# Decode of float64 weights: the low word moved to ScalarE, the scaled word moved to PSUM, two biases written as numbers

## The chip, the cores and the metric

One core of one Trainium2 chip runs the whole program. The metric is the device time of one execution in microseconds (us). The kernel before took 1444.06 us, the median of three runs (1442.41 to 1444.91).

## The reference

Three stages follow one another on 8192 tokens of width 192. The first is a convolution whose seven taps per head come from a softmax; the second is an MLP with a rational activation; the third is an MLP with a hard-swish. The four weight matrices reach the kernel as float64.

```
w = exp(weight_gen - max);  w = w / (sum(w) + 1e-9)          # 2 x 4096 x 8 heads x 7 taps
x = sum over 7 taps of w * x shifted                         # 8192 x 192
h = x @ w_in                                                 # 192 -> 2048
P = a0 + a1*h + a2*h*h + a3*h*h*h
Q = 1 + |b0|*|h| + |b1|*h*h
x = (P / (Q + 1e-6)) @ w_out                                 # 2048 -> 192
h = x @ w_in2                                                # 192 -> 2048
out = (h * clip(h + 3, 0, 6) / 6) @ w_out2                   # 2048 -> 192
```

## The kernel before

The tokens are cut into 32 blocks of 256, and each block's 2048 hidden columns into four groups of 4 x 128. So there are 128 steps ("sl" in the code), and one step holds a 128x1024 tile of h in PSUM. TensorE (PE) multiplies; the elementwise work of a step is shared by VectorE (DVE), ScalarE (ACT) and GpSimd (POOL). For the first MLP a matrix is split into a high and a low half, so that three or five matmuls make one product.

One step of the first MLP goes: `in1` (PE, twenty matmuls, L258), `act_u`, `act_w`, `act_l` (ACT, L280 to L292), `pool_q` (POOL, L299), `dve_t` and `dve_t2` (DVE, L303 and L307), `act_ln`, `act_exp`, `act_q` (ACT, L314 to L323), `dve_hi` (DVE, L328), `pool_m` (POOL, L336), `dve_d` (DVE, L341), `pool_lo` (POOL, L349), `out1` (PE). The second MLP is `in2` (PE), `act_r2` (ACT, L393, a Relu), `dve_g2` (DVE, L399), `out2` (PE, L415). Between the two stand `mid_y` (ACT, L227) and `mid_f` (PE, L237).

Before that, and woven into the first steps, 28 jobs bring the weights in. A job loads a piece as pairs of 32-bit words into a tile `st` (SP, L433), 512 or 384 words wide per partition. `dec_scale` (L458, ACT) multiplies the high words by a power of two into a tile `dt`; `dec_low` (L465, DVE) turns the low word into its top three bits; `dec_join` (L471, DVE) shifts `dt` and ors the three bits in; `dec_sign` (L478, DVE) ors the sign in and writes `wf` (or, for the last matrix, `wo` itself). For three of the four matrices a "cut" follows: ACT rounds the high half (L487) and POOL or DVE subtracts it (L488). The 28 jobs are 12 of 512 words ("in" and "pair") and 16 of 384 words ("o1" and "o2").

The order on each engine is written out by a planner, `plan()` (L708): every operation has an engine or a choice of two, a cost, a due time and buffers that it takes (`take`), and the planner lists what would start first. Each engine then runs its list in that order, and an instruction that waits holds up all behind it. Buffers are rings: three `st`, three `wf`, two `dt`, two `h1` and two `h2` tiles in PSUM. A `st` buffer comes free after the job's sign, and the next load waits for that. `h2` is the PSUM ring of the second MLP and also of the transposes `xT` and of `yf`. When all 28 jobs have ended, the space of `st`, `wf` and `dt` is given to the tiles of the second MLP (`to_late`, L76): nothing of the second MLP starts before.

Of the kernel before, what the change touches and what calls it, by code (L numbers as in the profile page):

```python
# [8 lines left out]
F32 = mybir.dt.float32  # L9
F32R = mybir.dt.float32r  # L10
I32 = mybir.dt.int32
U32 = mybir.dt.uint32
AF = mybir.ActivationFunctionType
ALU = mybir.AluOpType
# [5 lines left out]
def kernel(  # L20
# [12 lines left out]
    nc = tc.nc  # L33
    P = 128
# [8 lines left out]
    NTB = SUB * P  # L43
# [9 lines left out]
    CEPS = 1.0 + 1e-6  # L53
# [9 lines left out]
    const = ctx.enter_context(tc.tile_pool(name="const", bufs=1))  # L63
# [4 lines left out]
    ps_h2 = ctx.enter_context(tc.tile_pool(name="ps_h2", bufs=2, space=PSUM))  # L68
# [4 lines left out]
    early = [stage.enter_context(tc.tile_pool(name="early", bufs=1))]  # L73
# [8 lines left out]
    acol = const.tile([P, 4], F32, name="acol")  # L82
    bcol = const.tile([P, 2], F32, name="bcol")
    bab = const.tile([P, 2], F32, name="bab")
    ceps = const.tile([P, 1], F32, name="ceps")
    half = const.tile([P, 1], F32, name="half")

    win = [
        {n: wts.tile([P, FF], F32R, name=f"win{i}{n}") for n in ("hi", "lo")} for i in range(2)
# [221 lines left out]
    def act_ln(sl):  # L311
        e = e1[sl]
        r = two.tile([P, GW], F32, tag="r0", name="r0")
        nc.scalar.activation(out=r, in_=e["w"], func=AF.Ln, bias=ceps[:, 0:1])  # L314
        e["r"] = r

    def act_exp(sl):
# [60 lines left out]
    h2 = {}  # L378
# [10 lines left out]
    def act_r2(sl, hh):  # L389
        r = late[0].tile([P, 2 * NTB], F32, tag="r2", name="r2")  # L390
        h = h2[sl, hh]
        r2[sl, hh] = r
        nc.scalar.activation(out=r, in_=h, func=AF.Relu, scale=1.0 / 6.0, bias=half[:, 0:1])  # L393

    def dve_g2(sl, hh):
        r, h = r2.pop((sl, hh)), h2.pop((sl, hh))
# [60 lines left out]

    def dec_scale(j):  # L458
        st = j["st"]
        j["y"] = early[0].tile([P, st.shape[1]], F32, tag="dt", name="dt", bufs=2)  # L460
        nc.scalar.activation(
            out=j["y"], in_=st[:, :, 1].bitcast(F32), func=AF.Copy, scale=2.0 ** -112
        )

    def dec_low(j):  # L465
        low = j["st"][:, :, 0]
        nc.vector.tensor_scalar(
            out=low, in0=low.bitcast(U32), scalar1=2.0 ** -29, scalar2=7.0, op0=ALU.mult, op1=ALU.min
        )

    def dec_join(j):  # L471
# [61 lines left out]
    def job_step(key, n, e=None):  # L533
        eng = nc.vector if e == "DVE" else nc.gpsimd
        if n == "load":
            kind, a = key[0], key[1:]
            j = {"in": job_in, "pair": job_pair, "o1": job_out1, "o2": job_out2}[kind](*a)
            job_load(j)
            jobs[key] = j
            return  # L540
        j = jobs[key]
        if n == "scale":
            dec_scale(j)
        elif n == "low":
            dec_low(j)
        elif n == "join":
            dec_join(j)
        elif n == "sign":
            dec_sign(j)
        elif n == "hi":  # L550
            j["cuts"] = j["cuts"](j["w"])
            for h, _ in j["cuts"]:
                h()
        else:
            for _, l in j["cuts"]:
                if l:
                    l(eng)
# [18 lines left out]
    def op(key, eng, cost, prio, emit, after=(), take=(), lat=0.15):  # L576
        choice = eng if isinstance(eng, tuple) else ((eng, cost, 0.0),)
        ops[key] = dict(
            key=key, choice=choice, prio=prio, emit=emit, after=after, take=take, lat=lat
        )  # L580
# [12 lines left out]
    for n, key in enumerate(order):  # L593
        p = JP0 + n * JPT - (30.0 if n < 2 else 0.0)
        f64, split = WS == 2, key[0] != "o2"
        sz = 1.0 if key[0] in ("in", "pair") else 0.75
        last = ("job", key, "lo" if split else "sign" if f64 else "load")
        wf = [("wf", 3, [last])] if split else []

        def step(k, eng, cost, prev, take=(), lat=0.15, also=[]):  # L600
            op(
                ("job", key, k), eng, cost, LOADP.get((n, k), p - LP * (k == "load")), lambda e=None, key=key, k=k: job_step(key, k, e),
                ([("job", key, prev)] if prev else []) + also, take, lat,
            )

        flex = (("POOL", 1.25 * sz, 0.0), ("DVE", 0.62 * sz, PEN))
        step("load", "SP", 1.46 * sz, None, [("st", 3, [("job", key, "sign")])] if f64 else wf, 2.2)
        if f64:
            step("scale", "ACT", 0.52 * sz, "load", [("dt", 2, [("job", key, "sign")])])
            step("low", "DVE", 0.34 * sz, "load")  # L610
            step("join", "DVE", 0.61 * sz, "scale", also=[("job", key, "low")])
            step("sign", "DVE", 0.61 * sz, "join", wf)
        if split:
            step("hi", "ACT", 1.6 if key[0] == "pair" else 0.52 * sz, "sign" if f64 else "load")
            step("lo", flex, 0, "hi")
        done[key] = last
# [37 lines left out]
    for sl in range(NS):  # L654
# [3 lines left out]
        for k in range(2):  # L658
            jobs_in = [done["in", 0, q], done["pair", 0, q // 2 * 2]]
            add("in1", "PE", 1.09, t + k, in1, sl, k,  # L660
                after=[("lo0", b)] + jobs_in + prev("in1", k),
                take=[("h1", 2, [("dve_d", sl)])] if k == 0 else [])
            add("out1", "PE", 1.09, t + 2 * T + 2.2 + k, out1, sl, k,
                after=[("pool_lo", sl), done["o1", 2 * q + k]] + prev("out1", k),
                take=[("y1", 1, [("lo1h", b)])] if q + k == 0 else [])
            jobs_in = [done["in", 1, q], done["pair", 1, q // 2 * 2]]
            t2 = t + 6 * T + (4.3, 8.1)[k]
            add("in2", "PE", 1.09, t2, in2, sl, k, after=[("lo1t", b)] + jobs_in,
                take=[("h2", 2, [("dve_g2", sl, k)])])
            t2 = t + 6 * T + (5.5, T + 0.7)[k]  # L670
            add("act_r2", "ACT", 0.57, t2, act_r2, sl, k, after=[("in2", sl, k)],
                take=[("r2", 2, [("dve_g2", sl, k)])])
            t2 = t + 6 * T + (7.9, T + 1.3)[k]
            add("dve_g2", "DVE", 0.6, t2, dve_g2, sl, k, after=[("act_r2", sl, k)] + prev("dve_g2", k),
                take=[("g2", 2, [("out2", sl, 1)])] if k == 0 else [])
            add("out2", "PE", 1.3, t + 7 * T + 5.4 + k, out2, sl, k,
                after=[("dve_g2", sl, k), done["o2", 2 * q + k]] + prev("out2", k),
                take=[("y2", 1, [("evac", b)])] if q + k == 0 else [])
# [7 lines left out]
        add("dve_t", "DVE", 1.13, t + 5.6 - CH, dve_t, sl, after=[("act_l", sl)])  # L686
        add("dve_t2", "DVE", 1.2, t + 6.7 - CH, dve_t2, sl, after=[("dve_t", sl), ("act_u", sl)])
        add("act_ln", "ACT", 1.04, t + 6.95 - CH, act_ln, sl, after=[("pool_q", sl)],
            take=[("r0", 2, [("pool_lo", sl)])])
        add("act_exp", "ACT", 0.95, t + 8.1 - CH, act_exp, sl, after=[("act_ln", sl)])  # L690
# [67 lines left out]

    with tc.manual_schedule():
        nc.scalar.preload_act_table_set("natural_log_exp_and_others")  # L760
        nc.gpsimd.memset(ceps, CEPS)
        nc.gpsimd.memset(half, 0.5)
        make_identity(nc, ident)
        for e in range(2):
            nc.gpsimd.tensor_tensor(
                out=fold[:, e, :], in0=ident[:, 0:64], in1=ident[:, 64:P], op=ALU.add
            )
        for o, e in plan():
            o["emit"](*([e] if len(o["choice"]) > 1 else []))
# [30 lines left out]
```

## Time and profile before

| | |
|---|---|
| median of three runs | 1444.06 us |
| the profiled execution | 1442.11 us |
| its span in the trace | 1440.2 us |
| PE busy | 1316.6 us (91%) |
| DVE busy | 1210.5 us (84%) |
| ACT busy | 1050.1 us (73%) |
| POOL busy | 1009.3 us (70%) |

The profile divides the span into 40 slices of 36 us and gives each a digit, the busy share in tenths. In the first four slices PE has the digits 1, 3, 3 and 4, and DVE 6, 9, 9 and 9; from the fifth on PE has a 9 up to the last. The granted clock of TensorE has 9, 6, 5 and 7 in the first four slices and 9, which is full speed, from the fifth on. DMA moves 92 to 155 GB/s in the first four slices and little afterwards. The shares of the whole span say only that PE is the engine with the most to do; which engine sets the pace in the first part has to be read from that part alone.

### The profile page before, as it was taken

What the parts mean: (1) busy time and instruction counts of PE and PEld (TensorE: products, weight loads), DVE (VectorE), ACT (ScalarE), POOL (GpSimd) and SP (SyncE); (2) the same over time, 40 slices, a digit from 0 to 9 for tenths busy, and PEclk for the clock granted to TensorE, in tenths of its full rate; (3) what the DMA queues carried; (4) which work ended last, traced back from release to release, by engine and by line L of the source; (5) the groups of instructions that cost most, each with busy time, mean ns of one, the idle gap of its engine ahead of it and who ended that gap; (6) DMA issues with size and microseconds to landing.
All of it is one profiled execution on the core that took longest, in us unless ns stands there. A gap on an engine that the chain in (4) does not pass through costs nothing.

```text
span 1440.2 us, 23822 instructions
## 1 busy us (share of the span) xinstructions
PE 1316.6 (91%) x9920; PEld 1298.4 (90%) x9920; DVE 1210.5 (84%) x1168; ACT 1050.1 (73%) x1298; POOL 1009.3 (70%) x434
## 2 busy tenths in 40 slices
PE   1334999999999999999999999999999999999998
PEld 1334999999999999999999999999999999999998
DVE  6999889888888888889888888898888888988662
ACT  3656678787878777777787877777777777777772
POOL 4756676767676777677767776777777777777760
PEclk9657999999999999999999999999999999999999
DMA  6332001000010101001010100001010100000000
GB/s 155 95 104 92 28 7 37 7 10 33 2 37 7 37 7 37 6 4 35 6 37 7 37 6 10 29 6 37 7 37 6 35 9 1 6 7 7 6 7 12
DMA packets 15764, 37.96 MB, mean 26 GB/s; under 512 B 1832, under 2 KB 12072, under 8 KB 15656
## 3 DMA queue, kind: packets, MB, share of 16 engines
q1 hardware_dynamic: 15656, 36.44, 8.1%
q8 instruction: 78, 1.28, 0.4%
q14 instruction: 30, 0.25, 0.1%
HBM read 30.14 MB, written 6.29 MB: 25 GB/s over the span
## 4 chain that ended last, share of the span: by engine, by line
DVE 33%; POOL 25%; ACT 15%; issue 14%; PE 12%; DMA 1%; SPq 0%; POOLq 0%; DVEq 0%; ACTq 0%
POOL m L336 16%; POOL w L299 9%; DVE ghi L328 7%; PE h L258 6%; DVE h L307 5%; DVE g L399 5%; DVE m L341 4%; ACT r L319 4%; PE y L415 3%; DVE l L303 3%; ACT r L393 3%; DVE xc L176 3%; ACT l L292 2%; ACT u L280 2%; ACT w L323 2%
## 5 line engine op out<-in xcount | busy, mean ns | idle before, releaser
L336 POOL TENSOR_TENSOR m<-w,ghi 128x1024 f32<-128x1024 f32 x128 | 353.3, 2760 | 319.7 <-DVE ghi L328 237.8
L415 PE MATMUL y<-wo,g 128*128 128x192 f32 x2048 | 374.8, 325 | 0.0
L415 PEld LDWEIGHTS y<-wo,g 128*128 128x128 f32 x2048 | 329.5, 190 | 0.1
L299 POOL TENSOR_TENSOR w<-w,u 128x1024 f32<-128x1024 f32 x128 | 307.3, 2401 | 27.7 <-ACT w L285 27.7
L314 ACT ACTIVATE r<-w,ceps 128x1024 f32<-128x1024 f32 x128 | 147.4, 1152 | 230.5 <-POOL w L299 230.4
L349 POOL TENSOR_TENSOR glo<-m,r 128x1024 fp32r<-128x1024 f32 x128 | 308.9, 2413 | 9.3 <-DVE m L341 6.2
L258 PE MATMUL h<-xh,wst 128*128 128x256 f32 x1024 | 293.0, 286 | 0.1
L258 PE MATMUL h<-xl,wst 128*128 128x256 f32 x1024 | 292.2, 285 | 0.1
L341 DVE SCALAR_TENSOR_TENSOR m<-h,acol,m 128x1024 f32<-128x1024 f32 x128 | 164.0, 1281 | 144.2 <-POOL m L336 144.2
L393 ACT ACTIVATE r<-h,half 128x512 f32<-128x512 f32 x256 | 173.8, 679 | 52.9 <-PE h L258 52.7
L258 PE MATMUL h<-xh,win0hi 128*128 128x256 f32 x512 | 164.7, 322 | 46.2 <-DVE m L341 45.4
L258 PEld LDWEIGHTS h<-xh,wst 128*128 128x128 f32 x1024 | 199.2, 195 | 0.3 <-ACT xh L244 0.3
L258 PEld LDWEIGHTS h<-xl,wst 128*128 128x128 f32 x1024 | 199.1, 194 | 0.4 <-DVE xl L217 0.3
L399 DVE SCALAR_TENSOR_TENSOR g<-r,h 128x512 f32<-128x512 f32 x256 | 174.0, 681 | 26.2 <-ACT r L393 26.2
L328 DVE SCALAR_TENSOR_TENSOR ghi<-h,acol,r 128x1024 fp32r<-128x1024 f32 x128 | 163.8, 1279 | 17.8 <-ACT r L319 17.7
L176 DVE TENSOR_REDUCE xc<-prod 128x192 f32<-128x1344 f32 x64 | 166.6, 2604 | 0.0
L303 DVE TENSOR_TENSOR l<-h,l 128x1024 f32<-128x1024 f32 x128 | 155.7, 1217 | 10.6 <-ACT l L292 8.9
L307 DVE SCALAR_TENSOR_TENSOR h<-l,acol,h 128x1024 f32<-128x1024 f32 x128 | 164.0, 1282 | 0.6
L258 PE MATMUL h<-xh,win1hi 128*128 128x256 f32 x512 | 161.8, 316 | 0.5 <-DVE g L399 0.3
L285 ACT ACTIVATE w<-u,bab 128x1024 f32<-128x1024 f32 x128 | 159.4, 1245 | 0.0
L367 PE MATMUL y<-ghi,wo1h 128*128 128x256 f32 x512 | 157.6, 308 | 0.0
L292 ACT ACTIVATE l<-h,acol 128x1024 f32<-128x1024 f32 x128 | 154.3, 1205 | 2.3 <-DVE h L307 2.3
(75 smaller groups left out, 3210.7 us busy)
## 6 DMA issues: line engine op xcount, KB each, us to landing
x<-in_x_dram SPq DMA_DIRECT2D x14, 960.0 KB, 4.6
st<-in_moe_w_out_dram SPq DMA_DIRECT2D x16, 384.0 KB, 3.2
out_dram<-osb SPq DMA_DIRECT2D x32, 192.0 KB, 1.9
st<-in_moe_w_in_dram SPq DMA_DIRECT2D x8, 512.0 KB, 9.2
st<-in_moe_w_in_dram SPq DMA_DIRECT2D x8, 256.0 KB, 6.7
x<-in_x_dram SPq DMA_DIRECT2D x4, 472.5 KB
wg<-in_weight_gen_dram SPq DMA_DIRECT2D x16, 112.0 KB, 2.2
x<-in_x_dram SPq DMA_DIRECT2D x2, 3.0 KB
```

The source lines that it names most:

```text
L176: nc.vector.tensor_reduce(out=xc[b][:, s, 0:D], in_=prod.pop((b, s)).rearrange("p k h g -> p (h g) k"), axis=AX.X, op=ALU.add,)
L258: nc.tensor.matmul(out=dst, lhsT=l[:, fs], rhs=r, start=(n == 0), stop=(n == len(seq) - 1), skip_group_check=True,)
L299: nc.gpsimd.tensor_tensor(out=e["w"], in0=e["w"], in1=e["u"], op=ALU.mult)
L303: nc.vector.tensor_tensor(out=e["l"], in0=h, in1=e["l"], op=ALU.mult)
L307: nc.vector.scalar_tensor_tensor(out=h, in0=e["l"], scalar=acol[:, 1:2], in1=h, op0=ALU.add, op1=ALU.mult)
L328: nc.vector.scalar_tensor_tensor(out=fl(ghi), in0=h, scalar=acol[:, 0:1], in1=e["r"], op0=ALU.add, op1=ALU.mult)
L336: nc.gpsimd.tensor_tensor(out=m, in0=e["w"], in1=fl(g1[sl][0]).bitcast(F32), op=ALU.mult)
L341: nc.vector.scalar_tensor_tensor(out=e["m"], in0=h, scalar=acol[:, 0:1], in1=e["m"], op0=ALU.add, op1=ALU.subtract)
L349: nc.gpsimd.tensor_tensor(out=fl(glo), in0=e["m"], in1=e["r"], op=ALU.mult)
L393: nc.scalar.activation(out=r, in_=h, func=AF.Relu, scale=1.0 / 6.0, bias=half[:, 0:1])
L399: nc.vector.scalar_tensor_tensor(out=g2[sl][:, hh * 2 : hh * 2 + 2, :].rearrange("p f t -> p (f t)"), in0=r, scalar=1.0, in1=h, op0=ALU.mi ...
L415: nc.tensor.matmul(out=y2[b][:, s, :], lhsT=g[:, f, s * P : (s + 1) * P], rhs=wo2[:, n, :], start=(n == 0 and s == 0), stop=(n == NF - 1), ...
```

## The change

The multiplication of `dec_low` goes from DVE to ACT, as a Copy with a scale that rounds to the same three bits. Its scale holds the result under 7.5, so that no minimum is needed. `dec_scale` writes its result into a tile of the PSUM ring `h2` in place of the SBUF ring `dt`, which goes. The planner's table follows: `low` is now an ACT operation ahead of `scale`, and `scale` takes one of the two `h2` buffers until the job's sign. The biases of Ln and Relu are numbers in the instruction in place of a column in SBUF, and the two memsets that filled the columns go.

```
-        r = ... nc.scalar.activation(out=r, in_=e["w"], func=AF.Ln, bias=ceps[:, 0:1])
+        r = ... nc.scalar.activation(out=r, in_=e["w"], func=AF.Ln, bias=CEPS)
...
-        nc.scalar.activation(out=r, in_=h, func=AF.Relu, scale=1.0 / 6.0, bias=half[:, 0:1])
+        nc.scalar.activation(out=r, in_=h, func=AF.Relu, scale=1.0 / 6.0, bias=0.5)
...
     def dec_scale(j):
         st = j["st"]
-        j["y"] = early[0].tile([P, st.shape[1]], F32, tag="dt", name="dt", bufs=2)
+        j["y"] = ps_h2.tile([P, 2 * NTB], F32, tag="h2", name="dt")[:, : st.shape[1]]
...
     def dec_low(j):
         low = j["st"][:, :, 0]
-        nc.vector.tensor_scalar(
-            out=low, in0=low.bitcast(U32), scalar1=2.0 ** -29, scalar2=7.0, op0=ALU.mult, op1=ALU.min
+        nc.scalar.activation(
+            out=low, in_=low.bitcast(U32), func=AF.Copy, scale=0.936 * 2.0 ** -29
         )
...
-            step("scale", "ACT", 0.52 * sz, "load", [("dt", 2, [("job", key, "sign")])])
-            step("low", "DVE", 0.34 * sz, "load")
+            step("low", "ACT", 0.52 * sz, "load")
+            step("scale", "ACT", 0.52 * sz, "load", [("h2", 2, [("job", key, "sign")])])
...
-        nc.gpsimd.memset(ceps, CEPS)
-        nc.gpsimd.memset(half, 0.5)
```

The order that the planner makes moves with it. First DVE, in the middle of the weight decode, where the jobs of the matrix `w_out` are (L467 is low, L473 join, L480 sign; `wf` is the decoded weight). Before:

```order
L473 SCALAR_TENSOR_TENSOR dt<-dt,st 128x384
L467 TENSOR_SCALAR st<-st 128x384
L480 SCALAR_TENSOR_TENSOR wf<-st,dt 128x384
L473 SCALAR_TENSOR_TENSOR dt<-dt,st 128x384
L467 TENSOR_SCALAR st<-st 128x384
L480 SCALAR_TENSOR_TENSOR wf<-st,dt 128x384
L473 SCALAR_TENSOR_TENSOR dt<-dt,st 128x384
L142 TENSOR_REDUCE sg<-wg 128x32
```

DVE in the changed kernel, at the same jobs (L471 is join, L478 sign, L486 the subtraction of a cut):

```order
L471 SCALAR_TENSOR_TENSOR dt<-dt,st 128x384 x2
L478 SCALAR_TENSOR_TENSOR wf<-st,dt 128x384 x2
L471 SCALAR_TENSOR_TENSOR dt<-dt,st 128x384
L478 SCALAR_TENSOR_TENSOR wf<-st,dt 128x384
L486 TENSOR_TENSOR wo1l<-wf,wo1h 128x256
L486 TENSOR_TENSOR wo1s<-wf,wo1s 128x2x64
L486 TENSOR_TENSOR wo1l<-wf,wo1h 128x256
L486 TENSOR_TENSOR wo1s<-wf,wo1s 128x2x64
L326 SCALAR_TENSOR_TENSOR ghi<-h_254,acol,r_406 128x1024
```

The 28 lows are gone from DVE's list, and two cuts of `w_out` that POOL had are now here.

Second ACT, near the end of the decode, up to the first instruction of `mid_y`. Before (L461 is scale, L487 the rounding of a cut, L227 `mid_y`):

```order
L487 ACTIVATE win1hi<-wf 128x512
L461 ACTIVATE dt<-st 128x384
L314 ACTIVATE r_771<-w,ceps 128x1024
L280 ACTIVATE u<-h_706 128x1024
L319 ACTIVATE r_771<-r_771 128x1024
L323 ACTIVATE w<-w 128x1024
L285 ACTIVATE w<-u,bab 128x1024
L227 ACTIVATE ys<-y_431 128x256
```

ACT in the changed kernel (L465 is low, L459 scale, L485 the rounding of a cut, L225 `mid_y`):

```order
L485 ACTIVATE win1hi<-wf 128x512
L465 ACTIVATE st<-st 128x384
L459 ACTIVATE dt<-st 128x384
L312 ACTIVATE r_762<-w 128x1024
L465 ACTIVATE st<-st 128x384
L459 ACTIVATE dt<-st 128x384
L317 ACTIVATE r_762<-r_762 128x1024
L321 ACTIVATE w<-w 128x1024
L278 ACTIVATE u<-h_696 128x1024
L290 ACTIVATE l<-h_696,acol 128x1024
L283 ACTIVATE w<-u,bab 128x1024
L225 ACTIVATE ys<-y_419 128x256
```

A low now stands ahead of each scale, and the Ln has no column operand.

Third PE, at its first `mid_f`, which is the 210th row of its list both before and after. Before (L371 and L372 are the last matmuls of `out1`, L237 `mid_f`, L194 a transpose, L258 here the first product with `win1`):

```order
L371 MATMUL y_431<-glo,wo1h 128x256
L372 MATMUL y_431<-glo,wo1s 128x256
L237 MATMUL yf<-ys,fold 128x256
L194 MATMUL xT<-ident,xc 128x128
L195 MATMUL xT<-ident,xc 128x128
L194 MATMUL xT<-ident,xc 128x128
L195 MATMUL xT<-ident,xc 128x128
L258 MATMUL h_817<-xh,win1hi 128x256
```

PE in the changed kernel, the same place:

```order
L369 MATMUL y_419<-glo,wo1h 128x256
L370 MATMUL y_419<-glo,wo1s 128x256
L235 MATMUL yf<-ys,fold 128x256
L192 MATMUL xT<-ident,xc 128x128
L193 MATMUL xT<-ident,xc 128x128
L192 MATMUL xT<-ident,xc 128x128
L193 MATMUL xT<-ident,xc 128x128
L256 MATMUL h_810<-xh,win0hi 128x256
```

Up to this place PE's list is the same row for row; behind it a step of the first MLP now comes ahead of the first step of the second.

## Rows read from the trace of the kernel before

**Rows 1.** Stretches: length; busy (count) of PE, PEld, DVE, ACT, POOL; clock, DMA, GB/s.
```profile
25.00:134.90 109.90, 39.45 (x207) 37.06 (x207) 108.48 (x114) 63.85 (x96) 70.83 (x45) 0.69 0.34 103
134.90:200.00 65.10, 59.24 (x419) 57.29 (x420) 54.33 (x50) 46.62 (x57) 45.01 (x19) 0.92 0.06 19
200.00:1300.00 1100.00, 1081.43 (x8269) 1068.97 (x8268) 952.26 (x904) 843.32 (x1026) 805.80 (x321) 1.00 0.05 18
```

**Rows 2.** Timeline at the end of the decode: start us, us, instruction, idle before.
```profile
134.90 0.38 ACT L227 ACTIVATE ys<-y 128x256 f32<-128x256 f32 x1 [2.14 <-DVE wo L480]
...
135.33 1.22 PE L237 MATMUL yf<-ys,fold 128*128 128x256 f32 x2 [10.69 <-ACT ys L227]
```

**Rows 3.** Stretch 25 to 134.9 us: busy (count) of L467, L473, L480, L461 alone.
```profile
25.00:134.90 109.90, 24.69 (x25) 0.69 0.34 103
...
25.00:134.90 109.90, 21.41 (x26) 0.69 0.34 103
...
25.00:134.90 109.90, 24.93 (x26) 0.69 0.34 103
...
25.00:134.90 109.90, 14.41 (x25) 0.69 0.34 103
```

**Rows 4.** Timeline, DVE and POOL: lows, a join and a sign, free and held up.
```profile
5.82 0.43 DVE L467 TENSOR_SCALAR st<-st 128x512 int32<-128x512 uint32 x1 [5.82 <-DMA st<-in_moe_w_in_dram]
...
25.81 0.69 DVE L473 SCALAR_TENSOR_TENSOR dt<-dt,st 128x512 int32<-128x512 int32 x1
...
26.04 2.78 POOL L162 TENSOR_TENSOR prod<-x,wk 128x1344 f32<-128x1344 f32 x1 [7.37 <-DVE xc L176]
...
26.41 2.69 DVE L467 TENSOR_SCALAR st<-st 128x512 int32<-128x512 uint32 x1
...
120.85 2.58 POOL L299 TENSOR_TENSOR w<-w,u 128x1024 f32<-128x1024 f32 x1
...
121.09 2.74 DVE L480 SCALAR_TENSOR_TENSOR wo<-st,dt 128x384 int32<-128x384 int32 x1
```

**Rows 5.** Durations by line: ns min/median/max, first and last start; DVE.
```profile
L473 DVE SCALAR_TENSOR_TENSOR dt<-dt,st x28: 544/678/2736, 6.5 to 131.5; 128x384 int32<-128x384 int32 x16, 128x512 int32<-128x512 int32 x12
...
L307 DVE SCALAR_TENSOR_TENSOR h<-l,acol,h x128: 1268/1281/1291, 43.2 to 1395.8; 128x1024 f32<-128x1024 f32 x128
...
L399 DVE SCALAR_TENSOR_TENSOR g<-r,h x256: 658/679/707, 140.7 to 1433.3; 128x512 f32<-128x512 f32 x128
```

**Rows 6.** Waits of ACT, 25 to 134.9 us: us in total, times, longest.
```profile
ACT dt L461 <- DMA st<-in_moe_w_in_dram: 2.9, 2, 1.7
...
ACT xh L200 <- PE xT L195: 2.0, 2, 1.0
ACT u L280 <- PE h L258: 1.9, 1, 1.9
```

**Rows 7.** Durations by line: ns min/median/max; ACT.
```profile
L314 ACT ACTIVATE r<-w,ceps x128: 1132/1152/1159, 45.7 to 1398.1; 128x1024 f32<-128x1024 f32 x128
...
L323 ACT ACTIVATE w<-w x128: 1037/1047/1053, 48.2 to 1400.6; 128x1024 f32<-128x1024 f32 x128
...
L393 ACT ACTIVATE r<-h,half x256: 665/676/704, 140.0 to 1432.6; 128x512 f32<-128x512 f32 x128
...
L200 ACT ACTIVATE xh<-xT x32: 588/592/618, 27.2 to 1351.4; 128x512 fp32r<-128x512 f32 x32
...
L461 ACT ACTIVATE dt<-st x28: 529/560/697, 5.8 to 127.2; 128x384 f32<-128x384 f32 x16, 128x512 f32<-128x512 f32 x12
```

**Rows 8.** Waits of PE, 200 to 1300 us: us in total, times, longest.
```profile
PE yf L237 <- DVE g L399: 11.4, 27, 0.4
PE h L258 <- DVE m L341: 7.0, 24, 0.4
```

**Rows 9.** Waits of SP's queue, 0 to 140 us; then a load's time to landing.
```profile
SPq L433 <- DVE wf L480: 78.0, 17, 11.8
...
DMA to landing us min/median/max: 3.1/3.9/11.3
```

More of the change, by code (lines that the diff above doesn't have):

```diff
@@ L84 @@
     bab = const.tile([P, 2], F32, name="bab")
-    ceps = const.tile([P, 1], F32, name="ceps")
-    half = const.tile([P, 1], F32, name="half")
     win = [
@@ L313, in act_ln @@
         r = two.tile([P, GW], F32, tag="r0", name="r0")
-        nc.scalar.activation(out=r, in_=e["w"], func=AF.Ln, bias=ceps[:, 0:1])
+        nc.scalar.activation(out=r, in_=e["w"], func=AF.Ln, bias=CEPS)
         e["r"] = r
```

## The prediction

> **What bounds the kernel now.** I read the stretches first. From 200 to 1300 us PE is busy for 1081.43 of 1100 us at full clock, so there the matmuls set the pace and the other engines have slack [rows 1]. From 25 to 134.9 us it is another kernel: PE is busy for 39.45 of 109.9 us, and DVE for 108.48. DVE sets the pace of the weight decode, ACT with 63.85 us and POOL with 70.83 us wait for it [rows 1]. The end of this stretch is a sharp mark in the timeline: ACT's `mid_y` starts at 134.90 us, 2.14 us after it could have, released by the last sign of the decode, and PE's `mid_f` follows it after 10.69 us of waiting [rows 2]. Only from here on has PE both MLPs to work on. PE's list up to `mid_f` is the same in both kernels (the order ahead), so the matmuls left to do at this mark are the same, and a mark that comes earlier ends the program as much earlier, as long as PE then runs as it does now. The question is how long the stretch of 109.9 us becomes.
>
> **The change part by part.** *The lows leave DVE.* In the stretch 25 of the 28 stand, 24.69 us [rows 3], a mean of 0.99 us. That is not their work: a 512-wide low took 0.43 us at 5.82 us, and 2.69 us at 26.41 us, when POOL had begun a 2.78 us multiplication at 26.04 us [rows 4]. DVE's instruction ended just after POOL's did. All 24.69 us go.
>
> *The joins and signs lose their waits.* They have the same two faces: a join took 0.69 us at 25.81 us, a sign 2.74 us at 121.09 us, behind a POOL instruction of 2.58 us that began at 120.85 us [rows 4]. Both take two inputs from SBUF now. In the changed kernel one of the two lies in PSUM. The nearest rows for that are L307, with one input in SBUF, one in PSUM and its output in PSUM, and L399, with one of each and its output in SBUF. Over 128 and 256 instructions these never exceeded 1291 and 707 ns, while L473 ranges from 544 to 2736 [rows 5]. So I take the free time for all: 0.544 us for 384 words and 0.679 us for 512. Of the 26 joins in the stretch 16 are of 384 and 10 of 512 words: 16 x 0.544 + 10 x 0.679 = 15.5 us in place of 21.41, and the same 15.5 for the signs in place of 24.93 [rows 3]. The gain is 5.9 + 9.4 = 15.3 us. Its bounds are nothing, if an input in PSUM doesn't free them, and these 15.3 us.
>
> L399, with one input in PSUM, has a median of 679 ns, and the free join of the same 512 words, both inputs in SBUF, 0.69 us [rows 4, 5]: no surcharge. [...]
>
> *DVE's new sum.* 108.5 - 24.7 - 15.3 = 68.5 us. From the order, DVE's list up to the mark gains a 512-wide cut, four narrower ones and one `dve_d`, and loses two cuts of 64 partitions; with nothing above 1.3 us among them I add 1.5 us: 70 us. POOL stays near its 71 us; it gives up what DVE takes.
>
> *ACT's new sum.* A low has the shape and the strided read of a scale, and the 25 scales in the stretch took 14.41 us [rows 3]; 63.85 + 14.4 = 78.3 us. No row shows a ScalarE instruction that reads integers or writes every second word. Its bounds: 0.53 us, the shortest scale, and 1.05 us, the time of twice the elements in L323 [rows 7], which would add another 12 us. A scale that writes to PSUM has no row either; reading PSUM instead of SBUF stands between 0.59 us (L200) and 0.70 us (the longest L461) for 512 words [rows 7], so a gain or a loss of up to 2 us over the 25. I take the value of the scale for both.
>
> [...]
>
> *The new stretch.* ACT has the most to do now: 78.3 us, against 70 and 71. DVE could run at 99% because the others kept its inputs ready. ACT will not quite: its waits that DVE's load did not cause were 2.9 us for DMA and 2.0 and 1.9 us for PE [rows 6], 6.8 us, and I keep them. 78.3 + 6.8 = 85.1 us, so the mark comes 24.8 us earlier, at about 110 us. The first 25 us I leave as they are: they wait for loads and the first convolution.
>
> *The rings.* A load waits for the sign of the job three before it: 78.0 us of waits in SP's queue were for a `wf` sign [rows 9]. 25 jobs in 85 us are 3.4 us a job, so a `st` buffer may be held for 10.2 us. It needs 3.9 us of landing [rows 9] and four instructions of 0.55 to 0.7 us, 6.3 us together; nearly 4 us are left for waits. The scaled word and `xT` now share the two `h2` buffers, only for the two or so transposes in the stretch; I cost that at nothing.
>
> *The biases.* L314 with a column operand takes 1152 ns, L323 of the same size with a number as its bias 1047; L393 takes 676 and L200, of the same shape and without one, 592 [rows 7]. I take 0.1 us from each Ln and each Relu. Over 128 and 256 instructions that is 35 us of ACT, but ACT is not what PE waits for after 200 us: PE waits for DVE's `g` and `m`, 11.4 + 7.0 us at 51 places of at most 0.4 us [rows 8]. Where Relu or Ln is what held DVE up, 0.1 us comes off; at half of the 51 that is 2.5 us. The bounds are 0 and the whole 18.4. The two memsets stand ahead of any work and are worth nothing.
>
> *Sum.* The profiled execution took 1442.11 us, 1.95 us less than the median of the runs. 1442.1 - 24.8 - 2.5 = 1414.8 us, and 1.95 us on top for the median: 1416.8. I say 1416.
>
> **The rivals.**
> (a) *Waits of the in-order lists stay on ACT.* Of ACT's 109.9 - 63.85 = 46 us of idle time in the stretch [rows 1], half stays, since a job's chain is now low, scale, join, sign with ACT in the first two places, and a scale at the head of the list waits for an `h2` buffer. 78.3 + 23 = 101.3 us, 8.6 us gained: with the biases 1433. For it: three rings and three engines of nearly the same load. Against it: nearly all of these waits were for a DVE that had no time left.
> (b) *The change doesn't do what it says:* join and sign go on waiting for POOL from PSUM. DVE has 108.5 - 24.7 + 1.5 = 85.3 us, as much as ACT, and two full engines in a chain leave some 5 us of gaps: 90 us, 1422. Against it stands L307, which never waited.
> (c) *Better than forecast:* ACT without waits, 78.3 us, and all of PE's 18.4 us of waits go: 1444 - 31.6 - 18.4 = 1394.
> (d) *Slower.* All of ACT's 46 us are round trips (sign, load, landing, low) and none was DVE's load. Then ACT's 14.4 us of lows come on top: 78.3 + 46 = 124.3 us, 14.4 more than now, 1456 with 2.5 off. It decides from the point at which more than 31.6 of the 46 us stay. Against it: DVE was busy for 99% of the stretch, so there was next to no time in which all waited for a load.
>
> **How the numbers follow.** The forecast 0.58, (a) 0.20, (b) 0.08, (c) 0.09, (d) 0.05. 0.2% is about 3 us, what a measurement of this kernel can tell from no change. All but (d) and the worst of (a) are faster by more than that: faster 0.92, same 0.03, slower 0.05. The range goes from (c) at 1394 to just above (a), 1434, which also takes in 12 us for a slow low.
>
> **What would show it.** In the profile after, no DVE instruction of a join or sign over 0.75 us; the lows on ACT near 0.56 us; `mid_y` near 110 us; ACT the busiest engine between 25 us and the mark; Ln near 1.05 and Relu near 0.59 us; PE from the mark on as long as now. I am wrong if `mid_y` comes after 125 us, with ACT waiting in front of lows and scales, or if PE's stretch behind the mark becomes longer, since behind the mark its list is another.

## The result and the profile after

The changed kernel takes 1398.88 us (median of four runs, 1398.21 to 1399.57), the kernel before in the same comparison 1443.73. The ratio is 0.969, with a 95% interval from 0.9673 to 0.9706: 44.9 us faster. The forecast was 1416 us, faster by 28. The profiled execution took 1399.57 us; its span is 1397.8.

The page of the changed kernel: busy time of each engine, then 40 slices of the span.

```profile
PE 1311.3 (94%) x9920; PEld 1296.0 (93%) x9920; DVE 1168.2 (84%) x1142; ACT 1031.6 (74%) x1326; POOL 1002.8 (72%) x430
...
PE   1448999999999999999999999999999999999998
...
DVE  6988889988888898888889888888988888897662
ACT  4897777777777777776777777677777777777772
```

PE is in its 9s from the fifth slice on as before, but a slice is now 34.9 us long, and the fourth slice has an 8 in place of a 4. ACT, at 5 to 6 tenths in the second to fourth slice before, has an 8 and a 9 in the second and third now.

The end of the decode, in the timeline (start us, us, instruction, idle before); these rows answer to [rows 2].

```profile
101.74 0.55 DVE L478 SCALAR_TENSOR_TENSOR wo<-st,dt 128x384 int32<-128x384 int32 x1
...
104.91 1.25 ACT L283 ACTIVATE w<-u,bab 128x1024 f32<-128x1024 f32 x1
...
106.04 0.39 ACT L225 ACTIVATE ys<-y 128x256 f32<-128x256 f32 x1
...
106.48 1.22 PE L235 MATMUL yf<-ys,fold 128*128 128x256 f32 x2 [5.80 <-ACT ys L225]
```

The mark, `mid_y` on ACT, stands at 106.04 us in place of 134.90. The last sign no longer releases it: the sign ends near 102.3 us, and `mid_y` starts when the ACT instructions ahead of it are done.

The stretches cut at that mark (length; busy time and count of PE, PEld, DVE, ACT, POOL; clock; DMA share; GB/s), for [rows 1].

```profile
25.00:106.04 81.04, 37.71 (x208) 35.53 (x208) 72.37 (x88) 73.93 (x120) 66.20 (x43) 0.79 0.45 139
106.04:171.10 65.06, 62.18 (x450) 61.44 (x451) 55.61 (x53) 47.52 (x62) 50.33 (x22) 0.92 0.06 19
171.10:1257.60 1086.50, 1075.17 (x8235) 1063.80 (x8234) 946.24 (x902) 815.87 (x1022) 799.87 (x319) 1.00 0.06 18
```

The stretch from 25 us to the mark is 81.04 us in place of 109.9. ACT is busy for 91% of it, DVE for 89%, POOL for 82%. Behind the mark, the first 65 us hold 450 matmuls in place of 419, at the same granted clock of 0.92. From the mark to the end it is 1397.8 - 106.04 = 1291.8 us, before 1440.2 - 134.9 = 1305.3. So the 42.4 us between the two spans are 28.9 ahead of the mark and 13.5 behind it. In these 13.5 us PE's idle time behind the mark falls by 10.5 us, from 28.7 to 18.2.

Durations in the changed kernel, ns min/median/max, for [rows 5, 7]: joins and signs on DVE; lows, scales, Ln and Relu on ACT.

```profile
L471 DVE SCALAR_TENSOR_TENSOR dt<-dt,st x28: 548/568/701, 6.9 to 101.1; 128x384 int32<-128x384 int32 x16, 128x512 int32<-128x512 int32 x12
...
L478 DVE SCALAR_TENSOR_TENSOR wf<-st,dt x20: 546/679/692, 8.2 to 96.5; 128x512 int32<-128x512 int32 x12, 128x384 int32<-128x384 int32 x8
...
L465 ACT ACTIVATE st<-st x28: 533/570/704, 5.7 to 100.1; 128x384 int32<-128x384 uint32 x16, 128x512 int32<-128x512 uint32 x12
...
L459 ACT ACTIVATE dt<-st x28: 492/522/652, 6.3 to 100.6; 128x384 f32<-128x384 f32 x16, 128x512 f32<-128x512 f32 x12
...
L312 ACT ACTIVATE r<-w x128: 1041/1061/1065, 43.6 to 1355.8; 128x1024 f32<-128x1024 f32 x128
...
L391 ACT ACTIVATE r<-h x256: 573/588/614, 116.0 to 1390.4; 128x512 f32<-128x512 f32 x128
```

No join is above 0.701 us and no sign above 0.692, where both had reached 2.7 us. The low costs what a scale cost before (570 against 560 ns in the median). Ln and Relu are each 0.09 us shorter (1061 against 1152 ns and 588 against 676 in the median).

One statement ahead of the prediction is too strong: the Copy does not round every low word to the same three bits as before. A word that stood for 4.0 is now scaled to 3.74, and one that stood for 6.6 to 6.18; whichever way the conversion to an integer rounds, one of the two changes. This is a matter of the last bit of a weight and not of time.

PE's waits from 200 to 1300 us (us in total, times, longest), for [rows 8].

```profile
PE yf L235 <- DVE g L397: 5.8, 14, 0.4
PE h L256 <- DVE m L339: 4.5, 14, 0.8
```

They were 18.4 us at 51 places and are 10.3 us at 28.

### The profile page after: what moved, and what is told of

It is laid out like the page before. It is cut to its first block, busy times and chain, and to the rows that moved or that the text cites. A ratio compares the mean times of both kernels' runs of the same rounds, so it can differ in the third digit from the quotient of the medians.

```text
span 1397.8 us, 23832 instructions
## 1 busy us (share of the span) xinstructions
PE 1311.3 (94%) x9920; PEld 1296.0 (93%) x9920; DVE 1168.2 (84%) x1142; ACT 1031.6 (74%) x1326; POOL 1002.8 (72%) x430
## 4 chain that ended last, share of the span: by engine, by line
PE 44%; DVE 29%; POOL 13%; issue 7%; ACT 4%; DMA 1%; SPq 0%; POOLq 0%; DVEq 0%; ACTq 0%
PE h L256 21%; PE y L413 12%; POOL m L334 9%; DVE ghi L326 6%; DVE h L305 5%; DVE xc L174 5%; DVE g L397 4%; DVE m L339 4%; POOL w L297 3%; DVE l L301 3%; PE y L366 2%; PE y L369 2%; PE y L370 2%; PE y L367 2%; PE y L365 2%
## 5 line engine op out<-in xcount | busy, mean ns | idle before, releaser
L334 POOL TENSOR_TENSOR m<-w,ghi 128x1024 f32<-128x1024 f32 x128 | 349.7, 2732 | 303.2 <-DVE ghi L326 273.3
L312 ACT ACTIVATE r<-w 128x1024 f32<-128x1024 f32 x128 | 135.7, 1060 | 218.5 <-POOL w L297 218.4
L391 ACT ACTIVATE r<-h 128x512 f32<-128x512 f32 x256 | 150.6, 589 | 65.8 <-PE h L256 65.7
```

What stands on the lines that cost most here:

```text
L334: nc.gpsimd.tensor_tensor(out=m, in0=e["w"], in1=fl(g1[sl][0]).bitcast(F32), op=ALU.mult)
```

## The experiments

Each was timed beside the kernel before, and the ratios are to it. Where a kernel's waits are compared, they are those of PE from 200 to 1300 us, for DVE's `g` at `yf` and for DVE's `m`; waits of less than 0.15 us are not counted in them.

**The biases alone** (`e1_bias`): the kernel before with

```
-        nc.scalar.activation(out=r, in_=e["w"], func=AF.Ln, bias=ceps[:, 0:1])
+        nc.scalar.activation(out=r, in_=e["w"], func=AF.Ln, bias=CEPS)
...
-        nc.scalar.activation(out=r, in_=h, func=AF.Relu, scale=1.0 / 6.0, bias=half[:, 0:1])
+        nc.scalar.activation(out=r, in_=h, func=AF.Relu, scale=1.0 / 6.0, bias=0.5)
```

> The kernel before with the two biases as numbers and nothing else; its order is the same. The changed kernel is 44.9 us faster: its mark (mid_y) comes 28.9 us earlier and the rest behind the mark is 13.5 us shorter. Theory A: the rest comes from the biases, Ln and Relu 0.09 us shorter each, which take PE's waits for DVE down: about 1432 us. Theory B, the recorded forecast's size: the biases are worth 2.5 us (1441), and the rest comes from the other order of the steps behind the mark.

Measured: 1434.16 us, ratio 0.9931 (0.9917 to 0.9945), some 10 us faster. The mark is where it was, and PE's waits are close to those of the changed kernel (the profiled execution took 1431.08 us, 3.1 less than the median):

```profile
L225 ACT ACTIVATE ys<-y x32: 383/383/388, 134.3 to 1402.7; 128x256 f32<-128x256 f32 x32
```

```profile
PE yf L235 <- DVE g L397: 5.9, 14, 0.4
PE h L256 <- DVE m L339: 3.5, 12, 0.3
```

Theory A holds: the two numbers are worth some four times what I forecast (by the interval 8 to 12 us), and PE's small waits fall by about as much (18.4 us down to 9.4).

**The decode alone** (`e2_decode`): the changed kernel with both columns back, the reverse of the diff above.

> The changed kernel with both bias columns back; its order is that of the changed kernel. Theory A (biases carry what is gained behind the mark): about 1410 us. Theory B (the order carries it): about 1401 us. The mark near 106 us in both.

Measured: 1407.4 us, ratio 0.9751 (0.9737 to 0.9764), 36 us faster. The first row here is the mark, at 107.1 us, the others are PE's waits.

```profile
L227 ACT ACTIVATE ys<-y x32: 359/387/393, 107.1 to 1379.2; 128x256 f32<-128x256 f32 x32
```

```profile
PE yf L237 <- DVE g L399: 10.5, 25, 0.4
PE h L258 <- DVE m L341: 7.8, 26, 0.7
```

The waits are back at 18.3 us and the mark stays within 1 us. Theory A is closer, at 1410, but not all that is gained behind the mark comes from the biases: from the mark to the end this kernel's profile has 1405.7 - 107.1 = 1298.6 us, 6.7 less than before, with the columns in. Part of the 6.7 may be TensorE's clock. These are the 55 us that begin some 10 us behind the mark, first before, then here, then in the changed kernel:

```profile
145.00:200.00 55.00, 49.65 (x372) 48.39 (x371) 47.56 (x42) 39.90 (x46) 38.36 (x17) 0.97 0.06 22
```

```profile
117.07:172.13 55.06, 52.47 (x406) 52.01 (x405) 48.01 (x47) 42.37 (x51) 44.36 (x19) 1.00 0.07 23
```

```profile
116.04:171.10 55.06, 52.63 (x397) 52.16 (x397) 46.88 (x45) 39.73 (x51) 43.20 (x19) 0.97 0.07 23
```

The granted clock is 0.97 before and in the changed kernel: in both it falls once to 0.50, for 3.4 us (from 176.0 us before, from 129.7 us in the changed kernel), about when a wait of PE for `m` ends, of 2.6 and 2.4 us. In this profile it stays at 1.00. By these rows I estimate that this is worth 0.03 of 55 us, 1.7 us, which is half of the 3.4. PE's idle time in them falls from 5.4 to 2.6 us, and here as in the changed kernel it stays lower than before. The rest of the 6.7 us was not taken apart. The decode and the biases add up within the intervals: 36 + 10 is 46, and the whole change 45.

**The low alone on ScalarE** (`e3_low`), the scaled word left in SBUF:

```
-        nc.vector.tensor_scalar(
-            out=low, in0=low.bitcast(U32), scalar1=2.0 ** -29, scalar2=7.0, op0=ALU.mult, op1=ALU.min
+        nc.scalar.activation(
+            out=low, in_=low.bitcast(U32), func=AF.Copy, scale=0.936 * 2.0 ** -29
...
+            step("low", "ACT", 0.52 * sz, "load")
             step("scale", "ACT", 0.52 * sz, "load", [("dt", 2, [("job", key, "sign")])])
-            step("low", "DVE", 0.34 * sz, "load")
```

> The kernel before with the low alone on ScalarE; the scaled word stays in SBUF with its ring of two. Theory: joins and signs read two inputs from SBUF and go on waiting for GpSimd, means near 0.85 and 1.0 us and maxima above 2.5; DVE still has some 85 us in the stretch, the mark comes near 115 us, time 1424. Rival: the waits came with the low and go with it: no join or sign above 0.8 us, mark near 106, time 1412.

Measured: 1429.86 us, ratio 0.9909 (0.9894 to 0.9923). Joins, ns min/median/max, and the joins and signs among the groups of DVE in the first 140 us (busy us, mean ns | idle before), here and then in the kernel before:

```profile
L473 DVE SCALAR_TENSOR_TENSOR dt<-dt,st x28: 540/686/2946, 6.9 to 122.8; 128x384 int32<-128x384 int32 x16, 128x512 int32<-128x512 int32 x12
```

```profile
L473 DVE SCALAR_TENSOR_TENSOR dt<-dt,st 128x384 int32<-128x384 int32 (+1 forms) x28 | 30.6, 1104 | 10.2 <-ACT dt L461 10.2
L480 DVE SCALAR_TENSOR_TENSOR wf<-st,dt 128x512 int32<-128x512 int32 (+1 forms) x20 | 18.1, 914 | 0.8
...
L480 DVE SCALAR_TENSOR_TENSOR wo<-st,dt 128x384 int32<-128x384 int32 x8 | 12.8, 1614 | 0.1
```

```profile
L467 DVE TENSOR_SCALAR st<-st 128x384 int32<-128x384 uint32 (+1 forms) x28 | 27.5, 988 | 9.2 <-DMA st<-in_moe_w_in_dram 9.2
L473 DVE SCALAR_TENSOR_TENSOR dt<-dt,st 128x384 int32<-128x384 int32 (+1 forms) x28 | 22.8, 822 | 0.4 <-ACT dt L461 0.3
L480 DVE SCALAR_TENSOR_TENSOR wf<-st,dt 128x512 int32<-128x512 int32 (+1 forms) x20 | 18.4, 927 | 0.2
...
L480 DVE SCALAR_TENSOR_TENSOR wo<-st,dt 128x384 int32<-128x384 int32 x8 | 8.0, 1001 | 0.0
```

The rival falls: joins go on waiting. But my 1424 was too good as well. The waits did not stay with their instructions: a join now takes 1.10 us in the mean (0.82 before), and a sign of the last matrix 1.61 us (1.00 before), while the other signs stay at 0.91 (0.93). Summed by these means, joins and signs take 12.5 us more than before. The lows had waited for some 17 us: 27.7 us in all, less 0.34 us for each of 384 words and 0.43 for each of 512. So most of what the lows no longer wait comes back on joins and signs in this order. The edit moved the order too: DVE has four multiplications of the convolution in the first 140 us, 8.3 us, in place of two with 3.1. The mark comes at 125.8 us, DVE being busy for 99.49 of the 100.8 us from 25 us to it.

**The scaled word alone in PSUM** (`e4_psum`), the low left on VectorE:

```
-        j["y"] = early[0].tile([P, st.shape[1]], F32, tag="dt", name="dt", bufs=2)
+        j["y"] = ps_h2.tile([P, 2 * NTB], F32, tag="h2", name="dt")[:, : st.shape[1]]
...
-            step("scale", "ACT", 0.52 * sz, "load", [("dt", 2, [("job", key, "sign")])])
+            step("scale", "ACT", 0.52 * sz, "load", [("h2", 2, [("job", key, "sign")])])
```

> The kernel before with the scaled word in PSUM alone; the low stays on VectorE. Theory: joins and signs are free (none above 0.75 us), lows keep their waits near 1.0 us in the mean, DVE has 93 us, the mark comes near 119 us, time 1428. Rival: the waits for GpSimd move over to the lows (mean above 1.4 us) and the time stays above 1436.

Measured: 1425.36 us, ratio 0.9873 (0.9858 to 0.9888). Lows and joins:

```profile
L467 DVE TENSOR_SCALAR st<-st x28: 346/505/2506, 5.8 to 125.9; 128x384 int32<-128x384 uint32 x16, 128x512 int32<-128x512 uint32 x12
...
L473 DVE SCALAR_TENSOR_TENSOR dt<-dt,st x28: 548/567/718, 6.5 to 127.8; 128x384 int32<-128x384 int32 x16, 128x512 int32<-128x512 int32 x12
```

The theory holds in kind, and in the time (1428 expected): joins are free with one input in PSUM, lows go on waiting, at a mean of 1.07 us, little more than before (0.99). Joins and signs gave up some 15.5 us, and the lows took on 2.4: here hardly any of the waits moved over. The stretch was not what I expected: DVE is busy for 101.2 us ahead of the mark (93 expected), and the mark stands at 130.3 us (119 expected). It can't be set beside the others, since PE's list has 24 more rows ahead of it, and the program ends earlier by way of a shorter rest behind it (1294.5 us). The product of the two halves' ratios is 0.978, and both together have 0.975.

**One number each**: the changed kernel with one column back, Relu's (`e5_ln`) or Ln's (`e6_relu`).

```
+        nc.scalar.activation(out=r, in_=h, func=AF.Relu, scale=1.0 / 6.0, bias=half[:, 0:1])    # e5_ln
...
+        nc.scalar.activation(out=r, in_=e["w"], func=AF.Ln, bias=ceps[:, 0:1])                  # e6_relu
```

> The changed kernel with Relu's bias column back, so Ln alone has a number. Both numbers together took 1407.4 us (both columns) to 1398.9, 8.5 us. Theory A: each half carries its share, Ln by way of the chain Ln, Exp, dve_hi, pool_m, dve_d that frees an h1 buffer: about 1403. Theory B: Ln alone carries it all, 1399, since 1024 elements long ACT instructions hold the others up. Theory C: Ln is worth nothing, 1407, because POOL ahead of Ln sets that chain.

> The changed kernel with Ln's bias column back, so Relu alone has a number. Theory A: about 1403, PE's waits for DVE's g at yf fall from 10.5 to about 6 us in total. Theory B: 1407. Theory C: 1399.

Measured: 1404.44 us (0.9732, 0.9719 to 0.9745) and 1402.37 us (0.9721, 0.9708 to 0.9734). With neither it was 0.9751, with both 0.969. Theory A is the nearest in both: of 44.9 less 36.0, 8.9 us, Ln alone brings about 2.7 and Relu alone 4.3. The intervals are some 4 us wide, and that of Ln alone overlaps the one with neither, so the times don't show whether the 1.9 us that are left come only with both. The waits show more. Those for `m` fall from 7.8 us at 26 places to 4.7 at 14 with either number. Those for `g` fall to 9.7 and 8.6 us, not to the 6 that I expected of Relu; only both together bring them to 5.8. Here is the same `yf` in the middle of the program with neither number, with Ln's, with Relu's and with both:

```profile
686.61 0.45 PE L237 MATMUL yf<-ys,fold 128*128 128x256 f32 x1 [0.42 <-DVE g L399]
```

```profile
683.30 0.46 PE L236 MATMUL yf<-ys,fold 128*128 128x256 f32 x1 [0.36 <-DVE g L398]
```

```profile
684.15 0.45 PE L236 MATMUL yf<-ys,fold 128*128 128x256 f32 x1 [0.24 <-DVE g L398]
```

```profile
684.13 0.46 PE L235 MATMUL yf<-ys,fold 128*128 128x256 f32 x1
```

This wait falls from 0.42 us to 0.36, to 0.24, and to under 0.15. From 300 us on it goes so at nearly every second block; at the blocks between, the wait is 0.41 to 0.43 us in all four kernels.

**Which engine sets the pace now** (`e7_scale2`, `e8_sign2`): the changed kernel with each scale, or each sign, issued twice, writing the same values.

```
         nc.scalar.activation(
             out=j["y"], in_=st[:, :, 1].bitcast(F32), func=AF.Copy, scale=2.0 ** -112
         )
+        nc.scalar.activation(
+            out=j["y"], in_=st[:, :, 1].bitcast(F32), func=AF.Copy, scale=2.0 ** -112
+        )
```

> The changed kernel with each of the 28 scales issued twice, the second writing the same values: 28 x 0.45 to 0.55 us more on ScalarE, 14 us, in the same order. Theory: ScalarE sets the pace of the decode, the mark moves from 106 to 119 or 120 us, time 1411 to 1413. Rival: the chain of loads and waits or VectorE sets it and ScalarE's work lies beside it: less than 5 us, under 1404.

> The changed kernel with each of the 28 signs issued twice on VectorE, the second writing the same values: 28 x 0.47 to 0.6 us more, 14.5 us, in the same order. Theory (ScalarE alone sets the pace): under 1404. Rival: VectorE sets the pace as it did before: 1411 to 1414. If both this and the doubled scale cost 8 us or more, the two engines are linked so closely that either one's time comes through.

Measured: 1408.27 us (0.9767, 0.9754 to 0.9781) and 1407.24 us (0.9757, 0.9743 to 0.977), against the changed kernel 11 and 10 us slower by the ratios. The marks, first of the doubled scale, then of the doubled sign, each with its stretch up to the mark:

```profile
L225 ACT ACTIVATE ys<-y x32: 375/383/389, 118.6 to 1383.5; 128x256 f32<-128x256 f32 x32
...
25.00:118.60 93.60, 38.27 (x208) 35.71 (x208) 75.22 (x91) 89.20 (x148) 66.28 (x44) 0.77 0.39 124
```

```profile
L225 ACT ACTIVATE ys<-y x32: 378/384/392, 113.3 to 1378.8; 128x256 f32<-128x256 f32 x32
...
25.00:113.30 88.30, 37.79 (x208) 35.86 (x208) 84.74 (x113) 73.27 (x118) 65.09 (x43) 0.76 0.41 127
```

ACT's 15.3 us of extra work in the stretch move the mark by 12.6 us, DVE's 12.4 us by 7.3. But the profiled execution of the doubled scale took 1411.98 us, 3.7 more than the median, and by the medians the two cost the same, so which of them counts for more is not shown. Both expectations that only one counts fall, and the last sentence of the second holds in time: both cost 8 us or more, so either engine's time comes through. The same two runs show that the mark decides. From it to the end they have 1409.9 - 118.6 = 1291.3 and 1405.2 - 113.3 = 1291.9 us, and the changed kernel 1291.8: a mark that moves by 12.6 or 7.3 us moves the end by as much.

**The rings** (`e9_xt`, `e10_st4`, `e11_st4xt`): the first two transposes in an idle PSUM bank, so that the scaled words have `h2` to themselves; four `st` buffers in place of three; and both.

```
+        if b < 2:
+            ps = ps_y.tile([P, 2 * NTB], F32, tag="y2", name="xT")          # e9_xt, e11_st4xt
+        else:
+            ps = ps_h2.tile([P, 2 * NTB], F32, tag="h2", name="xT")
...
-    st = early[0].tile([P, n, 2], I32, tag="st", name="st", bufs=3)
+    st = early[0].tile([P, n, 2], I32, tag="st", name="st", bufs=4)         # e10_st4, e11_st4xt
...
```

> The changed kernel with the transposes of the first two blocks in the PSUM bank of y2, which is idle until the second MLP, so that the scaled words have both h2 buffers for themselves. In the changed kernel PE waits 31.5 us for a sign in front of xT, twice, 29.4 us the longest. Theory: those waits lie in a stretch in which PE has time, the mark stays near 106 us, time within 2 us of 1398.9. Rival: the shared ring holds the decode up: mark near 100 to 102, time 1393 to 1395.

> The changed kernel with four st buffers in place of three (the space of the old dt ring). ScalarE's waits for loads are 14.2 us over the first 140 us, most of them before 30 us, and SP's queue waits 55.6 us for a wf sign. Theory: the engines' own work sets the stretch, the loads are early enough; within 3 us of 1398.9, ScalarE busy for over 90% of the stretch either way. Rival: the ring of loads sets it, the mark comes 4 us or more earlier, time below 1395.

> Both of the last two changes together. Theory: the sum of the two, within 4 us of 1398.9. Rival: the two rings hide each other and only both together bring the mark to 98 to 100 us, time near 1392, which would be the fastest version here.

Measured: 1398.11 us (0.9681, 0.9668 to 0.9695), 1406.29 (0.9744, 0.9731 to 0.9757) and 1408.01 (0.9755, 0.9741 to 0.9768). Sharing `h2` costs nothing that can be measured: 0.9681 lies inside the interval of the changed kernel, with the mark at 105.7 us. A fourth `st` buffer makes it slower by some 8 us, which neither theory had. Its last sign and its mark:

```profile
L478 DVE SCALAR_TENSOR_TENSOR wo<-st,dt x8: 539/554/561, 75.9 to 106.0; 128x384 int32<-128x384 int32 x8
...
L225 ACT ACTIVATE ys<-y x32: 384/384/393, 110.2 to 1378.0; 128x256 f32<-128x256 f32 x32
```

The planner counts buffers too, and with a fourth it lists everything anew, so this run doesn't separate the ring from the order. The last sign starts at 106.0 us, 4.3 later than in the changed kernel, though more loads could be under way. DVE is busy for 78.0 us between 25 us and the mark, 5.6 more than in the changed kernel, and ACT for 73.8, as there; with both changes (`e11_st4xt`) DVE has 83.2. Why this order is the worse one was not settled. Of the versions run none is clearly faster than the changed kernel.

## Why the prediction was right, and where its sizes were off

*The size.* 24.8 + 2.5 = 27.3 us were forecast, and the spans differ by 42.4. Of the 15.1 us between, 4.1 lie ahead of the mark and 11.0 behind it.

*The mark decides, and PE's list ahead of it is the same.* Right: 28.9 of the 42.4 us lie ahead of the mark, 24.8 were forecast, and the doubled scales and signs show that a moved mark moves the end by as much.

*Lows leave, joins and signs lose their waits.* Right as a pair, and e4 shows that PSUM frees joins and signs by itself (none above 0.72 us, with the lows still on DVE). That the waits were for GpSimd (POOL) fits the whole trace before: all 21 lows, joins and signs of more than 0.9 us end 0.22 to 0.55 us after a POOL instruction does. DVE's sum came out at 72.4 us, forecast 70. Two readings in it were off: without the 25 lows DVE's instructions in the trace before cover 21.0 us less, not 24.69, since neighbours overlap (by some 0.08 us at each end of a low); and up to the mark DVE has as many `dve_d` as before and one `dve_t2` fewer, not one `dve_d` more. And lows and joins are not two independent terms as the working had them: in e3, with another order on DVE, most of the lows' waits came back on joins and signs (12.5 of some 17 us). Had only the lows moved, my sum would have been too good. In e4 little moved over the other way (2.4 of 15.5 us); what decides between the two was not tested.

*ACT's sum.* Forecast 78.3 us of work and 6.8 of waits, together 85.1; measured 73.93 and 7.1, together 81.04. The waits were right in sum, with some luck: those for loads are 4.3 us (2.9 forecast) and those for PE 1.7 (3.9 forecast). The work was 4.4 us too high. Taken alone, 25 lows took 14.8 us and 25 scales 13.7, but two ACT instructions in a row overlap in the trace by about 0.1 us (the timeline above the mark: 104.91 + 1.25 is 106.16, and the next starts at 106.04). Without the 25 lows ACT's instructions cover 62.8 us, so the lows add 11, not the 14.4 of the sum. The two-sided bound on writing PSUM resolved downwards: a scale is 0.04 us shorter in the median than in [rows 7].

*The biases.* This term was mis-sized: 2.5 us forecast, 8.9 measured beside the new decode and about 10 beside the old. The 0.09 us per instruction was right. What failed is the rule by which I turned it into time, 0.1 us off at half of the 51 places at which PE waits. Half of the places was right: 23 of the 51 are gone. But they lost some 0.35 us each and not 0.1: PE's waits fell by 8.1 us in total, and those that are left are as long as before (5.8 us at 14 places, 11.4 at 27). The four rows of `yf` show it at one place: 0.06 us off with Ln's number, 0.18 with Relu's, at least 0.27 with both, so one wait takes up the gain of several shortened instructions. Which ones, and by what chain, was not taken apart. The upper bound that I had put, 18.4 us, held it.

*PE behind the mark as long as now.* This step failed. Behind the mark the decode part alone saves 6.7 us with the bias columns in (e2's profile against that of before), some 1.7 of them by the clock, as I estimate. In the first 65 us behind it PE gets through 450 matmuls instead of 419. That comes with the decode part and not with the biases: with the numbers alone (e1) there are 421, with the decode alone (e2) 465. The planner's list has other steps there, and PE is idle for 2.9 us instead of 5.9; how the list brings this about was not taken apart. A mark that comes earlier is not all that a changed planner brings. I had named this as the place where I could be wrong, but had given it no term.

*The rivals.* (a), waits that stay on ACT, and (d), round trips, are out: ACT's idle time in the stretch fell from 46 to 7.1 us; of the 46, 40 had been waits for DVE. (b) is out by the maxima of joins and signs. The result lies between the forecast and (c), and nearer to (c), but not by its way: ACT's waits, which (c) had at nothing, stayed, and PE's fell by 8.1 of the 18.4 us. That the time came so near to (c) is in part luck, since ACT's shorter work and the gain behind the mark are in neither.

*PSUM as an input without a surcharge.* Right: the shortest join moved from 544 to 548 ns, and the longest is now 701, where a free one of 512 words took 0.69 us before. (The median fell from 678 to 568 because the waits went: the longest had been 2736.)

## What to carry to other kernels

Where an engine's instruction has two faces in the trace, 0.4 and 2.7 us, price the change by which instructions still have to wait behind another engine's, not by the mean. Moving one kind away can push most of its waits onto the next (some 12.5 of 17 us in e3) or hardly any (2.4 of 15.5 in e4), so the two kinds should be tried one by one. A short stretch in which PE starves can be worth more than the steady part of the program (here PE was busy for 39 of 110 us in it, and 28.9 of the 42.4 us came from it); find the instruction that ends it, and count the work ahead of it on each engine. And 0.1 us off an instruction that isn't on the busiest engine can still reach that engine (0.09 us off each Ln and Relu took PE's waits from 18.4 to 9.4 us in e1), and several of them can add up in one of its waits (at one `yf` 0.06 us came off with one number, 0.18 with the other, at least 0.27 with both).

## What the runs showed of the hardware that was not expected

With the lows gone from DVE the mean join rose from 0.82 to 1.10 us and the mean sign of the last matrix from 1.00 to 1.61 us, in an order that had changed with it. With joins and signs freed instead, the mean low rose only from 0.99 to 1.07. No join or sign with one input in PSUM took more than 0.72 us in the changed kernel or in e4, where those with both in SBUF reached 2.7 us before and 2.9 in e3. A ScalarE Copy that writes PSUM was a little shorter than one that writes SBUF (522 against 560 ns in the median). One that reads 32-bit integers from every second word and writes them back there was hardly longer than one that reads every second word and writes densely into SBUF (570 against 560).
